# Filler matmuls of 512 columns in place of 128, and the last output tile in three column parts

## The chip, the cores and the metric

One core of one Trainium2 chip. The metric is the device time of one execution in microseconds; a profiled execution also has a span, from its first to its last recorded instruction, some 1.3 us shorter. In the lines of a profile PE is TensorE (PEld its weight loads), DVE VectorE, ACT ScalarE, POOL GpSimd and SP SyncE; a q behind the name means the engine's sequencer. A store's landing is as the profile lists it.

## The reference, cut to what matters

One transformer block on 2048 tokens of width 640: a modulated layer norm, attention with 32 heads of 128 over cached keys and values, and a second branch with a token shift and an MLP.

```python
mod = (_silu(c) @ w_mod).reshape(c.shape[0], 6, 1, -1)         # six rows of 640
h = _layernorm(x) * (1 + ca) + sa
x = x + ga * attention(h, k_cache, v_cache, wq, wo)            # 32 heads, 2048 x 2048 scores
h = _layernorm(x) * (1 + cb) + sb
x = x + gb * mixer_mlp(h, w1, w2, w3, w4)                      # ends with @ w4 (1728 x 640)
```

## The kernel before

The kernel is written as a list of operations with estimated durations. A small list scheduler in Python puts them in an order for each engine and adds the semaphores. TensorE's order is fixed by keys; the other engines' orders follow the estimates.

Fillers: matmuls of ones by ones into a bank that nobody reads, so that TensorE is busy while the first loads arrive. They are meant to keep its clock up. In the trace of before the first thirty start 107 ns apart, from 1.08 us on, and the eight at 11.58 us start 56 ns apart.

```python
def dummy(e, n, t=None):
    for _ in range(n):
        ins = e.matmul((t or warm)[:, 0:128], ones_t[:], ones_t[:], start=True, stop=True)
...
spin(30, -300)          # before the transposition of c
...
spin(26, -298)          # before the modulation product
for k in range(KT):     # the modulation product, a filler after each column for k < 2
    ...
# step 0 of attention: spin(8), the first projection, spin(9), QK, spin(9)
```

The last matmuls, one tile of 128 tokens by 640 at a time, in two halves of 320 columns:

```python
for hf in range(2):
    for f in range(NF):                                    # NF = 14
        ... matmul(m[:, hf*512 : hf*512+HD], gT[f], w4[f][:, hf*HD:(hf+1)*HD])
    if last:                                               # tile 15: finish each half at once
        ... DVE: w = m * mod5;  DVE: o_ = w + b;  SyncE: store o_
```

The end of each engine's program. The body ends with a jump to a common block, where each engine loads a flag (was any value out of range?) and branches on it:

```python
for e, eng in names.items():
    run(e, 0, n)
    hint = eng.mark_branch_hint_location()
    run(e, n, self.FIRST[e])
    eng.br("fast").branch_hint(hint)          # the jump
...
    eng.wait_ge(self.flag_op.sem, self.flag_op.semval)
    eng.load(redo[eng.engine], flag[0:1, 0:1])
    ...
    eng.br_cmp(redo[eng.engine], 0, ..., on_true="done", on_false="general")
```

The hint marks a place some 47 us before the jump, where the trace shows a BRANCH_PREFETCH_HINT (in before at 1316.19 us, with TensorE's jump at 1363.84); no run here moved it, so what it does is not shown.

## Time and profile before

| | before |
|---|---|
| time, four runs | 1367.97 us median (1367.85 to 1371.74) |
| TensorE busy | 99% of the span |
| ScalarE busy | 81% |
| last matmul's end to end of span | 2.84 us |

How to read it: TensorE carries the whole span, so time can be gained at two ends only, before its stream is dense and after its last matmul. The prediction shows the lines. A second profile of the same kernel, taken later as a control (1367.96 us), has quicker start-up loads. TensorE's waits there:

```profile
PE f_S L440 <- POOL f_ones L403: 1.0, 1, 1.0
PE f_M L465 <- DMA f_W<-in_w_mod_dram: 0.4, 2, 0.3
PE f_S L806 <- ACT f_PQ L808: 0.4, 2, 0.2
```

The waits for the K and V loads (0.7 and 0.9 us in the prediction's fence) are absent, and the wait for the modulation weights is 0.4 us in place of 1.2.

### The profile page before, as it was taken

The page shows a single profiled execution, that of the slowest core. Times are in us where ns is not written, and L with a number is a line of the kernel's source. Part 1 is how long each engine was busy: PE and PEld are TensorE (multiplying, and loading weights), DVE is VectorE, ACT ScalarE, POOL GpSimd, SP SyncE. Part 2 cuts the span into 40 slices and gives each one's busy share as a digit, 9 for nine tenths or more (in the row PEclk, how much of TensorE's full clock was granted, in tenths as well). Part 3 has the DMA queues.
Part 4 walks back from the last instruction along what each step waited for, and adds up shares of the span by engine and source line. Part 5 has one row for each costly group of instructions (what it writes and reads, how often), then busy time and mean ns, then how long its engine had stood idle before and what let it go on. Part 6 is the DMA issues. An engine that isn't in the chain of part 4 may idle for free.

```text
span 1369.3 us, 29631 instructions
## 1 busy us (share of the span) xinstructions
PE 1349.0 (99%) x12841; PEld 939.4 (69%) x13075; DVE 574.7 (42%) x1440; ACT 1103.3 (81%) x1145; POOL 111.7 (8%) x97
## 2 busy tenths in 40 slices
PE   8999999999999999999999999999999999999999
PEld 6666777677677777677677777776776776655665
DVE  5554344544323332332333233233233345799553
ACT  6988888888888888888888888888888888833322
POOL 1000000000000000000000000000233237500000
PEclk9999999999999999999999999999999999999999
DMA  9642614272335221241205121422236110441210
GB/s 211 144 97 36 115 40 81 34 130 59 81 65 90 55 48 35 48 89 33 58 10 101 36 47 36 91 54 48 55 63 136 27 15 19 114 84 44 40 43 31
DMA packets 264787, 90.38 MB, mean 66 GB/s; under 512 B 244793, under 2 KB 262266, under 8 KB 264650
## 3 DMA queue, kind: packets, MB, share of 16 engines
q1 hardware_dynamic: 260682, 84.17, 30.9%
q0 software_dynamic: 672, 2.56, 0.9%
q10 hardware_dynamic: 3296, 1.67, 0.6%
q8 instruction: 104, 1.70, 0.5%
q14 instruction: 33, 0.27, 0.1%
HBM read 41.68 MB, written 2.63 MB: 32 GB/s over the span
## 4 chain that ended last, share of the span: by engine, by line
PE 96%; DMA 1%; issue 1%; DVE 1%; ACT 0%; POOL 0%; SPq 0%; POOLq 0%
PE f_O L825 35%; PE f_S L806 29%; PE f_M L729 10%; PE f_M L760 10%; PE f_S L1002 2%; PE f_M L1002 2%; PE f_O L989 2%; PE f_S L989 2%; PE f_S L940 1%; PE f_S L963 1%; PE f_M L963 1%; DMA f_KV<-in_A_v_cache_dram 1%; PE f_O L940 1%; DMA f_W<-in_w_mod_dram 1%; PE f_O L760 0%
## 5 line engine op out<-in xcount | busy, mean ns | idle before, releaser
L808 ACT ACTIVATE f_PQ<-f_S 128x1024 bf16<-128x1024 f32 x1024 | 1042.6, 1024 | 137.5 <-PE f_S L806 105.0
L825 PEld LDWEIGHTS f_O<-f_KV,f_PQ 128*128 128x128 bf16 x8192 | 634.8, 98 | 262.3 <-DVE f_small L517 1.4
L825 PE MATMUL f_O<-f_KV,f_PQ 128*128 128x129 bf16 x8192 | 796.4, 220 | 9.3 <-DMA f_KV<-in_A_v_cache_dram 0.9
L806 PE MATMUL f_S<-f_PQ,f_KV 128*128 128x512 bf16 x1831 | 650.8, 379 | 3.2 <-DMA f_KV<-in_A_k_cache_dram 0.7
L768 DVE TENSOR_TENSOR f_y<-f_M,f_y 128x320 f32<-128x320 f32 x192 | 94.4, 492 | 465.5 <-PE f_M L760 465.5
L760 PE MATMUL f_M<-f_wo,f_OO 128*128 128x320 bf16 x992 | 272.9, 299 | 0.0
L806 PEld LDWEIGHTS f_S<-f_PQ,f_KV 128*128 128x128 bf16 x2048 | 191.6, 98 | 13.4 <-ACT f_PQ L808 2.2
L729 PE MATMUL f_M<-f_hT,f_wq 128*128 128x512 bf16 (+1 forms) x635 | 189.0, 378 | 1.8 <-DVE f_tmp L771 0.2
L760 PEld LDWEIGHTS f_M<-f_wo,f_OO 128*128 128x128 bf16 x992 | 96.3, 98 | 28.5
L834 DVE TENSOR_TENSOR f_OO<-f_O,f_rl 128x256 bf16<-128x256 f32 x256 | 108.4, 423 | 8.3
L538 POOL TENSOR_TENSOR f_y<-f_y,f_mod 128x640 f32<-128x640 f32 x32 | 49.2, 1544 | 735.2 <-DVE f_y L768 735.1
L733 DVE CAST f_PQ<-f_M 128x512 bf16<-128x512 f32 x127 | 87.8, 692 | 50.7 <-PE f_M L729 49.5
L729 PEld LDWEIGHTS f_M<-f_hT,f_wq 128*128 128x128 bf16 x640 | 62.5, 98 | 49.8 <-DVE f_tmp L771 0.6
L832 DVE RECIPROCAL f_rl<-f_O 128x2 f32<-128x2 f32 x256 | 43.5, 170 | 69.1 <-PE f_O L825 58.2
L992 ACT ACTIVATE f_OO<-f_S 128x512 bf16<-128x512 f32 x28 | 16.7, 597 | 43.6 <-PE f_S L989 43.6
L766 DVE COPY f_y<-f_M 128x320 f32<-128x320 f32 x32 | 15.7, 492 | 57.6 <-PE f_M L760 57.6
L499 DVE BATCH_NORM_STATS2 f_small<-f_y 128x6 f32<-128x320 f32 (+1 forms) x72 | 32.3, 479 | 1.0 <-POOL f_y L538 0.9
L1002 PE MATMUL f_S<-f_KV,f_OO 128*128 128x320 bf16 x224 | 31.7, 299 | 0.0
L1002 PE MATMUL f_M<-f_KV,f_OO 128*128 128x320 bf16 x224 | 31.7, 299 | 0.0
L544 ACT ACTIVATE f_xn<-f_y,f_small 128x640 bf16<-128x640 f32 x10 | 9.1, 916 | 25.7 <-DVE f_small L523 25.7
L661 DVE TENSOR_REDUCE f_small<-f_tmp 128x1 f32<-128x640 f32 x20 | 16.4, 820 | 29.9 <-ACT f_PQ L808 29.9
L992 ACT ACTIVATE f_OO<-f_O 128x512 bf16<-128x512 f32 x28 | 16.7, 596 | 14.1 <-PE f_O L989 14.1
(148 smaller groups left out, 534.9 us busy)
## 6 DMA issues: line engine op xcount, KB each, us to landing
f_KV<-in_A_v_cache_dram SPq DMA_DIRECT2D x28, 512.0 KB, 4.7
f_wo<-in_A_wo_dram SPq DMA_DIRECT2D x8, 640.0 KB, 4.3
f_wq<-in_A_wq_dram SPq DMA_DIRECT2D x7, 640.0 KB, 4.9
f_xin<-in_A_x_dram SPq DMA_DIRECT2D x13, 320.0 KB, 3.5
out_dram<-f_xin SPq DMA_DIRECT2D x15, 160.0 KB, 1.8
f_KV<-in_B_w_dram SPq DMA_DIRECT2D x5, 432.0 KB, 3.6
f_KV<-in_A_k_cache_dram SPq DMA_TRANSPOSE x128, 2.7
f_OO<-f_OO SPq DMA_TRANSPOSE x128, 2.5
```

What stands on the lines that cost most here:

```text
L538: P.op(eng, lambda e: e.tensor_tensor(out=out, in0=a, in1=b, op=op), COST[eng][0], rd, wr, prio, lat=300 if eng == "POOL" else None, dual= ...
L729: P.op("PE", lambda e, i=i, kk=kk, mm=mm, a=a, z=z: e.matmul(mm[:, 0:z - a], wq_t[g % 2][:, kk, hh * 128:(hh + 1) * 128], hT_t[ch][:, kk, ...
L733: P.op("DVE", lambda e: e.tensor_copy(q.ap, m.ap), 690, (m,), (q,), s * NP - 90)
L760: P.op("PE", lambda e, m=m, qt=qt, hf=hf, hh=hh: e.matmul(m[:, 0:HD], OT_ap[gs][:, qt, hh, :], wo_t[g % 2][:, hh, hf * HD:(hf + 1) * HD], ...
L768: P.op("DVE", lambda e, m=m, yt=yt: e.tensor_tensor(out=yt.ap, in0=m[:, 0:HD], in1=yt.ap, op=ALU.add), 490, (m, yt), (yt,), s * NP - 60)
L806: P.op("PE", lambda e, sp=sp, r=r, kt=kt: e.matmul(sp[:, r * QC:(r + 1) * QC], K_ap[b][:, kt * 128:(kt + 1) * 128], q.ap, start=True, stop ...
L808: x = P.op("ACT", lambda e, sp=sp, pt=pt: e.activation(pt.ap.rearrange("p k q -> p (k q)"), sp.ap, ACT.Exp, scale=SCALE), 1021, (sp,), (pt ...
L825: ins = e.matmul(o[bk][:, w * 129:w * 129 + 129], pt[:, r, qt * 128:(qt + 1) * 128], V_ap[b][:, u, 0:129], start=(u == 0 and w == 0), stop ...
L832: P.op("DVE", lambda e, ov=ov, i0=i0: e.reciprocal(rl_t[:, i0:i0 + 2].unsqueeze(2), ov[:, 0:258].rearrange("p (u d) -> p u d", u=2)[:, :, ...
L834: evac.append(P.op("DVE", lambda e, ov=ov, i0=i0, bk=bk: e.tensor_tensor(out=On_ap[gs][:, 2 * bk:2 * bk + 2, hh, :], in0=ov[:, 0:258].rear ...
L989: P.op("PE", lambda e, m=m, f=f, kk=kk: e.matmul(m.ap, w3_ap[:, kk, f * 128:(f + 1) * 128], nT_ap[ch][:, kk, :], start=(kk == 0), stop=(kk ...
L1002: P.op("PE", lambda e, f=f, hf=hf: e.matmul(m[:, hf * 512:hf * 512 + HD], gT_ap[:, f, i * 128:(i + 1) * 128], w4_ap[f][:, hf * HD:(hf + 1) ...
```

## The change

Its intent: a filler of 512 columns keeps the array busy as long as four of 128, with a quarter of the instructions; and the last part of the last tile is smaller, so that less VectorE work and a smaller store follow the last matmul.

```diff
-            t_eng[e] = s + (o.dur if o.dma else max(o.dur - self.LAP.get(e, 0.0), 60.0))
+            t_eng[e] = s + (o.dur if o.dma or e == "PE" else max(o.dur - self.LAP.get(e, 0.0), 60.0))
...
-            ins = e.matmul((t or warm)[:, 0:128], ones_t[:], ones_t[:], start=True, stop=True)
+            ins = e.matmul((t or warm)[:, 0:512], ones_t[:], ones_t[:].unsqueeze(1).to_broadcast([128, 4, 128]), start=True, stop=True)
...
-    spin(30, -300)
+    spin(8, -300)
...
-    spin(26, -298)
+    spin(7, -298)
...
-                if k < 2:
+                if k < 2 and j % 4 == 3:
                     dummy(e, 1)
...
-            spin(8, -271)
+            spin(2, -271)
...
-            spin(9, -100, "O0")
-            spin(9, 1.5, "O1")
+            spin(2, -100, "O0")
+            spin(2, 1.5, "O1")
...
+        if last:
+            m3 = Tile(pool="T")
+            parts = ((m, 0, 0, HD), (m, 512, HD, 512), (m3, 0, 512, D))
+        else:
+            parts = ((m, 0, 0, HD), (m, 512, HD, D))
```

The rest of the diff renames the loop over halves to one over parts.

More of the change, by code (lines that the diff above doesn't have):

```diff
@@ L444, in spin @@
         t = Tile(pool=pool) if pool else warm
-        P.op("PE", lambda e: dummy(e, n, t), n * 56, (ones,), (t,), key)
+        P.op("PE", lambda e: dummy(e, n, t), n * 216, (ones,), (t,), key)
     mc, c_ps = Tile(pool="M"), Tile(pool="M")
-    spin(30, -300)
+    spin(8, -300)
     def spread(e):
@@ L466, in mcol @@
                                start=(k == 0 and j == 0), stop=(k == KT - 1), skip_group_check=True)
-                if k < 2:
+                if k < 2 and j % 4 == 3:
                     dummy(e, 1)
             return ins
-        P.op("PE", mcol, 2 * KT * (85 if k < 2 else 62), (wm[k], s_bf, ones), (mc,) + ((warm,) if k < 2 else ()), -290 + k, accum=True)
+        P.op("PE", mcol, 2 * KT * (72 if k < 2 else 62), (wm[k], s_bf, ones), (mc,) + ((warm,) if k < 2 else ()), -290 + k, accum=True)
     saT, caT = T(small(KT)), T(small(KT))
@@ L999, in w4_tile @@
         last = t == SQ // 128 - 1
-        for hf in range(2):
+        if last:
[3 more added lines that the diff above has]
+            parts = ((m, 0, 0, HD), (m, 512, HD, D))
+        for n, (mm, o, c0, c1) in enumerate(parts):
             for f in range(NF):
-                P.op("PE", lambda e, f=f, hf=hf: e.matmul(m[:, hf * 512:hf * 512 + HD], gT_ap[:, f, i * 128:(i + 1) * 128],
-                                                                 w4_ap[f][:, hf * HD:(hf + 1) * HD], start=(f == 0), stop=(f == NF - 1)),
-                     MM(HD), (gT[f], w4_of(f), w4b, pad2), (m,), key + hf + 0.01 * f, accum=True)
+                P.op("PE", lambda e, f=f, mm=mm, o=o, c0=c0, c1=c1: e.matmul(mm[:, o:o + c1 - c0], gT_ap[:, f, i * 128:(i + 1) * 128],
+                                                                             w4_ap[f][:, c0:c1], start=(f == 0), stop=(f == NF - 1)),
+                     MM(c1 - c0), (gT[f], w4_of(f), w4b, pad2), (mm,), key + n + 0.01 * f, accum=True)
             if last:
-                c0, c1 = hf * HD, (hf + 1) * HD
-                w, o_ = tmp[t % 2], xin[3 * hf]
-                P.op("DVE", lambda e, hf=hf, c0=c0, c1=c1: e.tensor_tensor(out=w[:, c0:c1], in0=m[:, hf * 512:hf * 512 + HD], in1=mod_t[5][:, c0:c1], op=ALU.mult),
-                     490, (m, mod[5][hf]), (w,), key - 1000)
-                P.op("DVE", lambda e, o_=o_, c0=c0, c1=c1: e.tensor_tensor(out=o_[:, c0:c1], in0=w[:, c0:c1], in1=b[:, c0:c1], op=ALU.add), 490, (w, b), (o_,), key)
+                w, o_ = tmp[t % 2], xin[(0, 3, 1)[n]]
+                P.op("DVE", lambda e, mm=mm, o=o, c0=c0, c1=c1: e.tensor_tensor(out=w[:, c0:c1], in0=mm[:, o:o + c1 - c0], in1=mod_t[5][:, c0:c1], op=ALU.mult),
+                     dve(c1 - c0), (mm,) + tuple(mod[5]), (w,), key - 1000)
+                P.op("DVE", lambda e, o_=o_, c0=c0, c1=c1: e.tensor_tensor(out=o_[:, c0:c1], in0=w[:, c0:c1], in1=b[:, c0:c1], op=ALU.add),
+                     dve(c1 - c0), (w, b), (o_,), key)
                 dma("SP", lambda e, o_=o_, c0=c0, c1=c1: e.dma_start(out2d[t * 128:(t + 1) * 128, c0:c1], o_[:, c0:c1]), 80, (o_,), (), key)
```

## The prediction

> **What bounds the kernel now.** I read the page's busy shares and slices first, to see which engine carries the span and where it does not; then what TensorE waited for; then the chain of waits at the two ends, because the change touches only the start-up and the last output tile.
>
> ```profile
> PE 1349.0 (99%) x12841; PEld 939.4 (69%) x13075; DVE 574.7 (42%) x1440; ACT 1103.3 (81%) x1145; POOL 111.7 (8%) x97
> PE   8999999999999999999999999999999999999999
> PEclk9999999999999999999999999999999999999999
> ```
>
> The first line gives busy microseconds per engine: TensorE (PE) is busy 99% of 1369.3 us, ScalarE 81%. In the slices only the first is below 90%, and the granted clock is never low. The kernel is one long matmul stream, so a change pays only if it shortens that stream, shortens an idle piece of it, or shortens what follows its last matmul. TensorE's waits for the whole span:
>
> ```profile
> PE f_M L465 <- DMA f_W<-in_w_mod_dram: 1.2, 3, 0.8
> PE f_S L440 <- POOL f_ones L403: 1.0, 1, 1.0
> PE f_O L825 <- DMA f_KV<-in_A_v_cache_dram: 0.9, 1, 0.9
> PE f_S L806 <- DMA f_KV<-in_A_k_cache_dram: 0.7, 1, 0.7
> PE f_S L806 <- ACT f_PQ L808: 0.4, 2, 0.2
> ```
>
> The columns are total us, times, longest. L465 is the modulation product, L440 the fillers, L806 and L825 the two attention products. The large waits are all start-up waits, and the releaser is a transfer or the first memset, none a filler. After 60 us the same view has three waits of 0.7 us in all; from 1230 us to the end it has none. The chain through the first 30 us:
>
> ```profile
> 2.62 7.54 DMA f_W<-in_w_mod_dram
> 10.16 0.05 issue
> 10.20 0.40 PE f_M L465 x10
> ...
> 17.05 0.86 POOL f_wq L619
> 17.91 0.02 issue
> 17.93 0.01 POOLq L252
> 17.95 9.90 DMA f_KV<-in_A_v_cache_dram
> 27.85 0.14 issue
> 27.99 0.61 PE f_O L825 x8
> ```
>
> (start us, length, what). Until 10.20 us the start-up is the load of the modulation weights; from 10.2 to 17 us it is a dependent sequence; from 17.95 to 27.99 it is the load of a V head. No filler stands in it. The chain at the other end:
>
> ```profile
> 1362.62 3.82 PE f_S L1002 x28
> 1366.44 0.02 issue
> 1366.46 0.50 DVE f_tmp L1008
> 1366.97 0.02 issue
> 1366.99 0.49 DVE f_xin L1010
> ```
>
> The last tile's 28 matmuls end at 1366.44, two VectorE operations of 320 columns follow until 1367.48, and then the store, issued at 1367.51 and (by the table of transfers) 1.6 us to landing, which takes us to the end of the span at 1369.3. What is serial after the last matmul is therefore 1.02 us of VectorE and about 1.8 us of store.
>
> [...] the first 30 fillers take 3.38 us from first start to last end, so (3.38 - 0.3)/29 = 106 ns apart; later 128-column matmuls are 56 ns apart (8 fillers in 0.61 us: (0.61 - 0.22)/7), and ten of 512 columns take 2.16 us in the chain, 216 ns each. [...] 492 ns at 320 columns, 824 ns at 640. [...] The trace shows the fixed part dominating: stores of 160 KB land in 1.8 us, of 80 KB in 1.6 us. [...]
>
> **Fillers, part by part.** Columns streamed: 30 x 128 = 3840 become 8 x 512 = 4096; 26 x 128 = 3328 become 7 x 512 = 3584; 20 x 128 = 2560 inside the modulation product become 4 x 512 = 2048; 8 x 128 become 2 x 512, the same; twice 9 x 128 = 1152 become twice 1024. In all 13056 become 12800, and 102 matmuls with their weight loads become 25. Where each lies in time:
>
> - First group, cold: 8 x 427 = 3.41 us in place of 30 x 107 = 3.20. The c-transpose behind it (4.32 us in the timeline) starts about 0.2 us later, and so does the small chain to the bf16 vector, which was complete at 5.73 + 0.17 = 5.90. Its user, the first modulation product, started at 7.33 when its weights landed. 1.2 us of the 1.4 us slack stay. The VectorE work behind that chain also moves by up to 0.2 us; the last normalised tile is done at 8.57 + 1.47 = 10.04 and its transposes began at 11.30, so that is hidden too.
> - Second group: before, 2.01 us from 4.54, ending at 6.55 (part cold, part warm). After, from about 4.75: perhaps two cold and five warm, 0.85 + 1.08 = 1.9 us, ending near 6.7. The wait for the weights ends at 7.33. Hidden.
> - Inside the product: before, 20 pairs at 81 ns, 1.6 us, done by about 9.1. After, 20 products at 26 ns ((0.65 - 0.16)/19 from the 20 that follow without fillers) plus 4 x 216 = 1.38 us. The 0.2 us gained turn into waiting, since the next product waits for its weights until 9.29, and the last until 10.20.
> - The group at 11.58: 2 x 216 = 432 ns in place of 448; the projection behind it starts at 12.16, when VectorE has its first input ready at 11.56 + 0.55 = 12.11. Hidden.
> - The groups at 13.52 and 15.03: 432 in place of 504 ns each. The first is followed by QK, which waits for ScalarE's copy of q until 13.72 + 0.38 = 14.10, with fillers done at 14.02 before and 13.95 after; the second by QK at 15.88, released by the exponentials. Hidden.
>
> Sum on the path: 0.0 us. Even a gain before 17 us would have to bring the V load forward to last; it could at most be some 0.05 us.
>
> **The last tile.** Matmuls: 14 each of 320, 192 and 128 columns. 320 costs 3.80/28 = 135.8 ns in the chain; 128 about 56 (12 of 129 columns in 0.68 us in the chain); 192 by the line through these, 82.6. Sum 14 x (135.8 + 82.6 + 56) = 3.84 us against 3.80: +0.04 us. So weight loads do not bind at 128 columns: the PV stream already runs at that rate with new weights every time. [...] VectorE must be free for it: part one ends at 1365.58 as now; part two is ready at 1364.54 + 14 x 0.0826 = 1365.70 and takes 2 x 0.357 + 0.04 = 0.75 us, to 1366.47; part three's matmuls end at 1366.48. It just fits. The buffers are free: the third bank was last read by the activations that ended at 1351.85, and its output row was read by a store issued at 1361.43. The store falls from 80 to 32 KB; by the two sizes above that is an estimated -0.1 us, but its rows are 256 B[...], so I count 0. Sum of the tail: -0.36 us.
>
> **The scheduler line.** TensorE's estimated time per operation loses its floor of 60 ns. TensorE's own order is sorted by key and does not move. The only short ones are 20 transposes (58 ns, 40 ns in all) and the 14 new small ones, beside the changed estimates of the fillers. That can only flip near ties in the order of the other engines. I count 0, with a small spread either way.
>
> Sum: 1368.05 - 0.36 + 0.0 = 1367.7 us.
>
> **Rivals.**
> (1) The fillers are on the path: a quarter as many instructions free TensorE's queue, or bring the warm clock earlier, and the start-up gets shorter by up to 1 us or so (1367). For it: the first slice is the only one below 90%. Against: every wait there names a transfer or the first memset, and the fillers end before the waits do.
> (2) The clock warms later, or drops again, since the filling inside the modulation product is now in four lumps. Then transposes, projection and first QK run cold: some 2 us of matmuls between 10.2 and 16 doubled, +2 us at worst (1370). Against: the lumps are as dense, and the gaps of 0.6 us are not longer than now.
> (3) The tail gives its gain back: three stores on one queue. One of the two last stores took 1042 ns to issue, the other 333. If the middle of three takes that long from about 1366.5, the last is issued near 1367.6, later than now, and the tail gains nothing or loses 0.1 us (1368.1).
> (4) A flipped order on VectorE or ScalarE makes TensorE wait in the middle. A few waits of 0.2 to 1 us would make +1 to +3 us (1370). Against: the same rules still give nearly the same order, and ScalarE has 19% to spare. A gain by such flips is bounded by the 0.7 us of waits there.
>
> **Range and chances.** The three times before are 1367.85, 1368.05 and 1371.74: the spread of runs is ten times the effect. A range from 1366.3 to 1370.2 holds rivals 1 to 3, most of 4, and a median that meets one high run. Two per cent would be 27 us, which nothing here comes near.
>
> **What would show it.** Right: the first slice's waits still name the modulation weights, K and V loads, with the same times at 10.20 and 27.99 within 0.2 us; the fillers show as 25 matmuls; the last VectorE operations are of 128 columns, near 290 ns each, and the time from last matmul to end is about 0.4 us shorter. Wrong: a TensorE wait behind VectorE or ScalarE that was not there, a first QK later than 14.2 us, matmuls at 427 ns for 512 columns after 6 us, or a last store whose issue waits for the one before. The prediction fails if start-up changes by over 1 us or new waits in the middle exceed 2 us.

The sum came to 1368.05 - 0.36 + 0.0 = 1367.7 us, the -0.36 being +0.04 for the matmuls, -0.40 for VectorE behind the last part and 0 for the store. An estimate from the traced operations gives the same: a line through VectorE's 492 ns at 320 columns and 824 at 640 puts 128 columns at 293 ns, so 2 x 0.293 + 0.04 = 0.63 us in place of 1.02. The changed kernel's trace has 292 and 291 ns, and 358 and 359 for the 192 columns that are counted as 0.357 us. "Cold" means the pitch of the first fillers: 107 ns in before, and in after 427 ns for 512 columns up to 4.0 us, then 216 to 226 from 4.73 on. That filling brings the clock up and pauses lower it, on which rivals 1 and 2 rest, is not shown. Nor had any run then shown that rows of 256 B are slow; that became rival R below.

## The result, and the profile after

The changed kernel is correct: 1368.59 us median (1368.34 to 1370.47, four runs) against 1367.97 (1367.85 to 1371.74). The ratio is 1.0001, with a 95% interval of 0.9982 to 1.002: the same. Ratios here are the mean time of one kernel's fast runs over that of the other's fast runs of the same rounds, so not quite the ratio of the medians.

The forecast was 1367.7 with a range from 1366.3 to 1370.2, so the total is inside. But the quick runs of after (1368.34, 1368.47, 1368.71) lie some 0.6 us above those of before (1367.85, 1367.88, 1368.05), where 0.36 less was expected. TensorE's waits after:

```profile
PE f_S L440 <- POOL f_ones L403: 1.0, 1, 1.0
PE f_M L465 <- DMA f_W<-in_w_mod_dram: 0.6, 1, 0.6
PE f_S L806 <- ACT f_PQ L808: 0.5, 2, 0.3
PE f_M L963 <- ACT f_PQ L950: 0.3, 1, 0.3
PE f_S L806 <- ACT f_PQ L737: 0.3, 1, 0.3
PE f_M L729 <- DVE f_tmp L771: 0.2, 1, 0.2
```

No K or V load is waited for, as in the control of before. The chain at the end (start us, length, what):

```profile
1360.01 3.06 PE f_S L1008 x28
1363.06 0.80 PE f_O L1008 x14
1363.86 0.03 issue
1363.89 0.02 DVEq L252
1363.91 0.04 issue
1363.95 0.30 DVE f_tmp L1013
1364.26 0.02 issue
1364.28 0.29 DVE f_xin L1015
```

The last part is there: 14 matmuls in 0.80 us, two VectorE operations of 0.3 us. The last one ends at 1364.57, which is 0.73 us after the last matmul's end (1363.84), against 1.05 before. Yet the span ends at 1367.02, 3.17 us after the last matmul, against 2.84. The time is lost in the store. First before, then after, the instructions that write the output tensor, with the times that their issue took (min/median/max, ns):

```profile
L1011 SPq DMA_DIRECT2D out_dram<-f_xin x2: 333/688/1042, 1365.6 to 1367.5; - x2
DMA to landing us min/median/max: 1.6/1.6/1.6
```

```profile
L1017 SPq DMA_DIRECT2D out_dram<-f_xin x3: 332/332/1159, 1363.0 to 1364.6; - x3
```

And the view of the transfers of after, from 1362 us to the end: the instruction queue (packets, MB, share of 16 engines' time), then the stores that were issued (KB each, us from issue to landing):

```profile
q8 instruction: 1, 0.02, 0.8%
...
out_dram<-f_xin SPq DMA_DIRECT2D x1, 48.0 KB, 2.6
out_dram<-f_xin SPq DMA_DIRECT2D x1, 32.0 KB, 2.3
```

The last store took 1.6 us to land before and 2.3 us now, though it is smaller. Both kernels have one store whose issue took over 1 us. Before it was the last but one, with 0.9 us to spare; after, it is the last one. And there is one packet of 16 KB on the instruction queue (q8) in this window. The packet records of the trace put it at 1364.43 and let it last 1.01 us. Of the 128 row packets of the second store, 120 left between 1364.70 and 1365.00; the other 8 left from 1365.43, when the big packet was done, to 1365.77. Eight of 128 rows are the share of one of the 16 DMA engines that the profile counts; the records do not name the engine. The issue of the third store ended at 1365.76 and its rows left from 1366.25. By these times, then, the packet that carries instructions stood in front of the second store on one engine, and the third store stood behind the second.

Where does such a packet come from? The profile puts it on the instruction queue. The 16 KB packets of that queue lie a median of 254 traced TensorE instructions apart in before and 253 in after (near the end of before at 25529, 25785, 26038), so I take each for a block of some 256 instructions of TensorE's code. That is an estimate from the spacing. But the last packet breaks the rhythm. In before it comes after 26213 instructions, 0.71 us after TensorE's jump to the common block has finished; in after 0.74 us after it. That jump takes 0.37 us in before and 1.09 in after, where a regular packet had started 1.6 us ahead of it, 2.83 us before the last matmul's end.

**Theory L.** The length of TensorE's code decides where its packets fall. With 77 filler matmuls and 77 weight loads fewer and 28 instructions more at the end (126 in all) a regular packet falls close to the jump, the jump waits for it, and the packet behind the jump falls among the last stores. **Rivals.** F: the wide fillers themselves cost time at the start. R: rows of 384 and 256 bytes are slow stores in themselves. N: all of it is noise.

### The profile page after: what moved, and what is told of

It reads as the page before. It is cut to its first block, busy times and chain, and to the rows that moved or that the text cites. A ratio compares the mean times of both kernels' runs of the same rounds, so it can differ in the third digit from the quotient of the medians.

```text
span 1367.0 us, 29510 instructions
## 1 busy us (share of the span) xinstructions
PE 1348.4 (99%) x12778; PEld 934.7 (68%) x13012; DVE 574.7 (42%) x1442; ACT 1102.6 (81%) x1145; POOL 111.5 (8%) x97
## 3 DMA queue, kind: packets, MB, share of 16 engines
q0 software_dynamic: 672, 2.56, 0.8%
## 4 chain that ended last, share of the span: by engine, by line
PE 97%; issue 1%; DMA 1%; DVE 1%; ACT 0%; SPq 0%; DVEq 0%
PE f_O L825 35%; PE f_S L806 29%; PE f_M L729 10%; PE f_M L760 10%; PE f_M L1008 2%; PE f_O L989 2%; PE f_S L989 2%; PE f_S L1008 2%; PE f_S L940 1%; PE f_S L963 1%; PE f_M L963 1%; PE f_O L940 1%; DMA f_W<-in_w_mod_dram 0%; DMA f_hT<-f_xn 0%; PE f_S L760 0%
## 5 line engine op out<-in xcount | busy, mean ns | idle before, releaser
L1008 PE MATMUL f_S<-f_KV,f_OO 128*128 128x320 bf16 (+1 forms) x224 | 31.0, 296 | 0.0
L1008 PEld LDWEIGHTS f_M<-f_KV,f_OO 128*128 128x128 bf16 x224 | 21.9, 98 | 8.9
```

The lines of the kernel that those rows point to most:

```text
L1008: P.op("PE", lambda e, f=f, mm=mm, o=o, c0=c0, c1=c1: e.matmul(mm[:, o:o + c1 - c0], gT_ap[:, f, i * 128:(i + 1) * 128], w4_ap[f][:, c0:c1 ...
```

## The experiments

Twelve runs in three groups (ten new kernels and the two old ones again); each group ran on one chip, with runs of before between its own. All are correct. The table has the timed runs, and from each run's one profile the numbers that the argument needs. "Jump" is how long TensorE's jump took, "packet" when the 16 KB packet behind it started, from the end of the last matmul. "Store" is the last store: issue and landing, both in us from its start. "Tail" is last matmul's end to end of span.

| kernel | TensorE instr. | jump | packet | store | tail | time: median (range) | ratio to before, interval |
|---|---|---|---|---|---|---|---|
| before (first profile) | 26230 | 0.37 | -1.51 | 0.33, 1.61 | 2.84 | | |
| after (first profile) | 26104 | 1.09 | +0.58 | 1.16, 2.27 | 3.17 | | |
| before_again | 26230 | 0.36 | -1.51 | 0.33, 1.62 | 2.85 | 1370.34 (1367.96 to 1371.68) | 1.0002, 0.9988 to 1.0017 |
| after_again | 26104 | 0.94 | +0.41 | 1.37, 2.48 | 3.38 | 1369.87 (1368.84 to 1372.11) | 1.0002, 0.9988 to 1.0017 |
| tail_only | 26258 | 0.36 | -0.18 | 0.83, 1.94 | 2.85 | 1369.73 (1367.60 to 1371.87) | 0.9994, 0.9980 to 1.0009 |
| fill_only | 26076 | 3.71 | +2.47 | 0.33, 3.40 | 4.63 | 1369.15 (1368.39 to 1370.58) | 0.9995, 0.9981 to 1.0009 |
| fill_pad | 26224 | 0.38 | -1.49 | 0.33, 1.60 | 2.83 | 1368.19 (1368.04 to 1369.69) | 0.9990, 0.9977 to 1.0003 |
| before_pad | 26328 | 0.37 | -1.51 | 0.33, 1.60 | 2.83 | 1370.49 (1369.41 to 1372.22) | 1.0005, 0.9991 to 1.0018 |
| after_pad | 26252 | 0.37 | +0.23 | 0.77, 1.89 | 2.79 | 1367.71 (1367.50 to 1368.82) | 0.9986, 0.9974 to 0.9999 |
| after_late | 26105 | 0.99 | +0.47 | 1.45, 2.56 | 3.53 | 1368.81 (1368.53 to 1371.17) | 0.9992, 0.9979 to 1.0004 |
| before_pad2 | 26332 | 2.21 | +0.47 | 0.33, 1.60 | 2.83 | 1369.85 (1368.81 to 1370.22) | 1.0003, 0.9990 to 1.0016 |
| after_late2 | 26105 | 0.46 | +3.65 | 0.33, 1.45 | 3.49 | 1371.11 (1368.99 to 1373.99) | 1.0015, 1.0000 to 1.0030 |
| after_pad_late2 | 26253 | 0.37 | +3.45 | 0.33, 1.45 | 3.39 | 1368.76 (1368.47 to 1371.62) | 1.0003, 0.9989 to 1.0016 |
| split416 | 26224 | 0.37 | -0.71 | 0.33, 1.53 | 2.56 | 1368.17 (1367.38 to 1368.98) | 0.9994, 0.9981 to 1.0007 |

The instructions are those recorded in the trace. The traces of the last group hold 234 matmul records that the earlier ones lack (before has 13075 weight loads and 12841 recorded matmuls on its page); they are left out of the count here. The three groups' runs of before (11 each) had medians of 1370.03, 1370.27 and 1369.32, with single runs from 1367.54 to 1374.59.

Three things are read off at once. First, from the 65th exponential of attention to the last matmul's end every one of the 14 profiles has between 1281.34 and 1281.40 us. So nothing that any kernel here does costs or gains in the middle, and the flipped orders that the prediction feared don't exist in a size that matters. Second, all differences are in the tail (2.56 to 4.63 us) and in the start-up, up to the 65th exponential (82.0 to 86.6 us), and the start-up varies between runs of one kernel (2.6 us between the two profiles of before) by more than the tail varies between kernels (2.1 us). So the timed intervals, some 0.15% or 2 us wide to each side, do not settle the tail. The profiles do. Third, where the jump is long, it ends 2.4 to 2.8 us after the start of a regular packet (after, after_again, fill_only, after_late, before_pad2). In after_late2 such a packet had started 5.1 us before the jump, and the jump took 0.46 us. So in these profiles the jump is long where a regular packet starts less than 2 us before it or while it lasts.

One part of the start-up's spread is the clock. In before_pad the record shows half the clock from 10.44 to 13.86 us, and the transposes there start 107 ns apart, against 56 ns in the other 13 profiles; it has the latest 65th exponential of all. Of the runs with a recorded clock, 5 of 56 with narrow fillers and 5 of 50 with wide ones have a mean below 1.000, so nothing ties this to the fillers. What brings it about stays open.

### First group: the parts of the change apart

**before_again and after_again**: the two kernels unchanged.

> The kernel before, unchanged, as a control and for a second profile (its first profile fell in a run with slow start-up loads: weights landed at 10.16 us, against 9.14 in the profile of the changed kernel). All theories: ratio 1.000, fast runs near 1367.9 us, some runs 2 to 4 us longer. With quick start-up loads the span should be near 1366.6 us; the time from TensorE's last matmul to the end of the span should again be 2.84 us, and the last store again 1.6 us from issue to landing.

> The changed kernel, unchanged. In the first comparison its quick runs (1368.34, 1368.47, 1368.71) were some 0.55 us above the quick runs of before (1367.85, 1367.88, 1368.05), where I had forecast 0.36 below. If that is noise between sessions (rival), the sign is not repeated. If it is real: +0.3 to +0.7 us between quick runs. The theory of the tail: the last store again takes about 1.1 us to issue and 2.3 us to landing, the time from last matmul to the end is again about 3.17 us.

The tails repeat: 2.85, and 3.38 with a last issue of 1.37 us. The times decide nothing: the changed kernel's median lies 0.2 us below that of the eleven runs of before and 0.5 us below before_again's, while its quickest run lies 0.9 us above before_again's (1368.84 against 1367.96), all behind a start-up that spreads over 3 us. So rival N is not excluded for the difference in times; the difference in the tail repeats.

**tail_only**: the last tile in three parts, fillers of 128 columns as before.

```diff
-            ins = e.matmul((t or warm)[:, 0:512], ones_t[:], ones_t[:].unsqueeze(1).to_broadcast([128, 4, 128]), start=True, stop=True)
+            ins = e.matmul((t or warm)[:, 0:128], ones_t[:], ones_t[:], start=True, stop=True)
```

and the counts of fillers, and the scheduler line, as in before.

> The last tile in three parts, fillers and scheduler line as before. Theory T (the tail): TensorE's last two branches now come later against its last matmul, the 16 KB packet [...] (1.0 to 1.4 us on one DMA engine) falls among the last stores, the third store's issue stalls; so last matmul to end about 3.2 us in place of 2.84, and +0.3 to +0.5 us in the quick runs. Rival F (the fillers cost the time): -0.4 to 0.0 us. Rival R [...]: the same +0.3 us as theory T, but with an issue of 0.33 us and a landing of 2.3 us for the last store.

This expectation and those of the second group give the 16 KB packet behind the jump to TensorE's final branch. That was a guess from its place in the trace; after_late refutes it below. My expectation for the tail missed: it is 2.85 us, as before's. The jump is as quick as before's, the packet starts 0.18 us before the last matmul's end, and the last store takes 0.83 us to issue and 1.94 to land. The packet stands among its stores all the same: 8 rows of the first and 8 of the second left only from 1368.89 us on, when it was done. So the three parts alone gain nothing and lose nothing: what VectorE saves, the store gives back. Only with the wide fillers does the tail get longer.

**fill_only**: the wide fillers and the scheduler line, with the last tile in two halves.

```diff
-            parts = ((m, 0, 0, HD), (m, 512, HD, 512), (m3, 0, 512, D))
+            parts = ((m, 0, 0, HD), (m, 512, HD, D))
```

> The wide fillers and the scheduler line, the last tile in two parts as before. Theory T: tail as before (2.84 us from last matmul to end), time within 0.15 us of before in the quick runs. Rival F: +0.2 to +0.6 us, with a start-up that is longer in the chain (first QK later against the landing of the last modulation weights than before, where they are 3.9 to 4.0 us apart).

Missed again, and this run taught the most. Not one line at the end differs from before, and yet the tail is 4.63 us. The chain at the end, and then the transfers from 1358 us on (packets of the instruction queue; the last two stores with KB and median landing):

```profile
1360.27 3.82 PE f_S L1002 x28
1364.09 0.02 issue
1364.11 0.50 DVE f_tmp L1008
1364.61 0.02 issue
1364.64 0.49 DVE f_xin L1010
```

```profile
q8 instruction: 2, 0.03, 1.0%
...
out_dram<-f_xin SPq DMA_DIRECT2D x2, 80.0 KB, 3.4
```

The chain is that of before, instruction by instruction. What differs is the second fence: two instruction packets in the window from 1358 us on, and a last store that lands after 3.4 us. A regular packet started at 1362.45, after the jump had begun (1361.49); the jump ended at 1365.20, 2.75 us after that packet's start; the packet behind the jump lasted from 1366.54 to 1367.47, and 8 of the last store's 128 rows left only at 1367.46, over 1 us after the other 120. So with other fillers, all issued before 16 us, the end comes 1.8 us later after the last matmul in this profile; theory L puts that down to the length of the code, which the next group tests. One profile does not show that every run of fill_only has this tail. The shortest of its six spans is 1367.1 us; less 1281.34 for the middle and 4.63 for the tail, that would leave 81.1 us of start-up, and no profile here has less than 82.0. By this estimate the tail of that run was at most 3.8 us. Rival F's path, a longer start-up, is not what happened: the first exponential starts at 13.80 us, against 14.00 in before_again.

### Second group: the length of the code alone

**fill_pad, before_pad, after_pad**: idle instructions on TensorE, one by one before operations in the attention stream, where they turn out to cost nothing (the middle keeps its 1281.34 to 1281.40 us). They wait for a semaphore that has long been reached.

```diff
+                if e == "PE" and a == 0 and k >= 1000 and (k - 1000) % 20 == 0 and (k - 1000) // 20 < 154:
+                    for by in ("POOL", "DVE")[:1 if waits[o] else 2]:
+                        eng.wait_ge(sems[by], 1)
```

(By the traces' counts 148 instructions are added in fill_pad and after_pad, 98 in before_pad with 102 in place of 154.)

> Wide fillers, last tile in two parts, and 148 idle wait instructions spread one by one over TensorE's attention stream, so that its code is again about as long as before's. Theory L (code length decides where TensorE's 16 KB instruction packets fall): the last packet but one falls again some 190 instructions before the end, the jump at the end takes 0.36 us (fill_only: 3.71), the packet of the final branch comes 1.5 us before the last matmul, the last store lands in 1.6 us, last matmul to end 2.85 us (fill_only: 4.63). At the start, as in fill_only: first packet near 14 us, last modulation weights near 9.05 us, first exponential near 13.8. Time: below before by 0.2 to 2 us, as before's start-up is slow or quick. Rival (the wide fillers themselves spoil the tail, say by the clock or the order of other engines): tail stays near 4.6 us.

> The kernel before, nothing of the change, only 98 idle wait instructions more in TensorE's attention stream, which brings the next packet boundary to some 20 to 50 instructions before the end, as in fill_only. Theory L: the jump at the end takes 1 to 3.7 us, the final branch's packet comes 0.4 to 2.5 us after the last matmul, among the last stores; last matmul to end 3.2 to 4.7 us in place of 2.85; time +0.3 to +1.9 us. Start-up as before: first packet at 8.6 to 9.5 us. Rival (packets have nothing to do with it): tail 2.85, time as before.

> The changed kernel with 148 idle waits more on TensorE, so with the wide fillers' start-up and with tail_only's place of the packets. Theory L: jump 0.36 us, final branch's packet 0.2 us before the last matmul's end, last store issue 0.83 and landing 1.94 us, tail 2.85 (after: 3.17 and 3.38). So 0.3 to 0.5 us below the changed kernel, and below before by 0.2 to 2 us. Rival: tail as in after.

fill_pad came out as expected: tail 2.83 against 4.63 in fill_only, jump 0.38 against 3.71, and no other line of the kernel differs from fill_only (the two ran in different groups, on different chips). Its transfers from 1358 us on:

```profile
q8 instruction: 1, 0.02, 0.4%
...
out_dram<-f_xin SPq DMA_DIRECT2D x2, 80.0 KB, 1.6
```

So neither the fillers' own work nor the scheduler line, which fill_pad has too, makes the long tail. after_pad is shorter too, as expected: 2.79 against 3.17 and 3.38. It is also the only kernel whose interval lies below 1 (0.9974 to 0.9999), 0.14% faster than before in that group; among twelve such intervals, one that just misses 1 may be chance. before_pad missed: its tail is 2.83, with no regular packet near the jump. It was four instructions short, since fill_only's 26076 plus a block of 256 (25529 to 25785 in before) is 26332 and it had 26328.

**after_late**: TensorE's final branch waits for the last three stores.

```diff
             eng.load(redo[eng.engine], flag[0:1, 0:1])
+            if e == "PE":
+                for o in [o for o in self.seq["SP"] if o.dma][-3:]:
+                    eng.wait_ge(o.sem, o.semval)
```

> The changed kernel, but TensorE's final branch waits until the last three stores have landed, so that the packet it fetches cannot fall among them. Theory C (the packet holds up the stores): last store issue 0.33 us, landing 1.4 to 1.6 us, last matmul to end 2.3 to 2.6 us in the profile, in place of 3.17 and 3.38; measured time below the changed kernel by 0.5 to 0.8 us if the late packet hides behind the end of the program, else no gain. Rival R (rows of 384 and 256 bytes are slow in themselves): last store still 2.0 to 2.5 us to landing.

A wrong idea of mine fell here: the packet still came 0.47 us after the last matmul and the tail was 3.53 (the last store landed at 3.31; TensorE's own final branch ends the span). The packet does not belong to the final branch. In the kernels of these groups it follows the end of the jump to the common block, by 0.7 to 0.9 us, 1.1 in after_pad and split416 and 1.34 in fill_only. This run says nothing of rival R.

### Third group: the mirror, the packet out of the way, and another split

**before_pad2**: before_pad with 102 idle instructions in place of 98.

> As before_pad, but with 102 idle waits on TensorE in place of 98. before_pad showed no packet near the end; fill_only (26076 traced TensorE instructions) did, and 26076 + 256 = 26332, four more than before_pad's 26328. With 102 the count is 26332. Theory L (the length modulo 256 decides): the tail of fill_only, without any part of the change: jump at the end 2.5 to 3.7 us (before 0.36), the packet behind it 1 to 2.5 us after the last matmul, last matmul to end 3.2 to 4.7 us (before 2.85). Rival: 2.85 again. Start-up as before's.

Half right. Four instructions more, and a regular packet is there (2.77 us before the last matmul's end), the jump takes 2.21 us in place of 0.37, and the packet behind it comes 0.47 us after the last matmul in place of 1.51 before it. No part of the change is in this kernel. But the tail stays 2.83: the packet ended at 1366.86, before the last store's rows left at 1367.33. So theory L holds for the jump and the packet; whether the stores suffer depends on a gap of half a microsecond, which I had not worked out.

**after_late2 and after_pad_late2**: the waits stand before the jump.

```diff
+            if e == "PE":
+                for o in [o for o in self.seq["SP"] if o.dma][-3:]:
+                    eng.wait_ge(o.sem, o.semval)
             eng.br("fast").branch_hint(hint)
```

> As after_late, with the waits put before TensorE's first jump, since after_late showed that the packet follows that jump by 0.7 us, not the final branch. Theory C (the packet holds up the last stores): none among them now; last store issue 0.33 us, landing 1.4 to 1.6 us, last matmul to the end of SyncE's stream 2.3 to 2.5 us; the profile's span may then end with TensorE's own jump and flag load, some 1 us after the landing. Measured time: below the changed kernel by up to 0.8 us if the end of the program doesn't wait for TensorE, above it by up to 1 us if it does. Rival R (short rows are slow): landing still above 2 us.

> after_late2 with the 148 idle waits of after_pad. Stores as in after_late2; TensorE's jump takes 0.36 us, its end comes some 1 us after the last landing. If the program's end waits for it, 0.0 to 0.5 us above after_pad, else 0.3 us below it.

The instructions of after_late2 that write the output tensor, with the times of their issue, and then its transfers from 1358 us on, with KB and landing:

```profile
L1020 SPq DMA_DIRECT2D out_dram<-f_xin x3: 332/332/333, 1364.8 to 1366.4; - x3
```

```profile
out_dram<-f_xin SPq DMA_DIRECT2D x1, 48.0 KB, 1.5
out_dram<-f_xin SPq DMA_DIRECT2D x1, 32.0 KB, 1.5
```

All three issues take 0.33 us, and rows of 384 and of 256 bytes land in 1.5 us. That settles rival R for these stores: the short rows do not land later. SyncE's stream ends 2.35 us after the last matmul, 0.5 us less than in before, which is what the change was made for (and 0.8 to 1.0 less than the changed kernel's 3.17 and 3.38). But TensorE's late jump now ends last (3.49), and the times are no better: 1371.11 with a slow start-up, and 1368.76 with the padding, against 1368.17 for split416 in the same group. The end waits for TensorE: where SyncE's stream ends last, the measured time is 1.32 to 1.41 us longer than that stream in the profile; here it is 2.70 us longer than SyncE's stream, and 1.57 us longer than TensorE's.

**split416**: two parts of 416 and 224 columns, wide fillers, 148 idle instructions.

```diff
-            parts = ((m, 0, 0, HD), (m, 512, HD, 512), (m3, 0, 512, D))
+            parts = ((m, 0, 0, 416), (m, 512, 416, D))
```

> The wide fillers, last tile in two parts of 416 and 224 columns, and 148 idle waits. [...] last store 1.6 us from issue to landing, packet 1.1 to 1.2 us before the last matmul's end and so ahead of the last store: last matmul to end 2.6 to 2.7 us. Against after_pad (2.79): 0.1 to 0.2 us less, against before 0.2 in the tail and 0.2 to 2 us in the start-up. It may be the fastest of all kernels here.

The chain at the end of its profile:

```profile
1359.70 3.82 PE f_S L1010 x28
1363.51 0.02 issue
1363.54 0.40 DVE f_tmp L1015
1363.94 0.02 issue
1363.96 0.39 DVE f_xin L1017
```

VectorE's part after the last matmul is 0.85 us (0.82 was expected), the store of 56 KB lands in 1.53 us, the packet (from 0.71 us before the last matmul's end, 0.93 us long) is over before the last store's rows leave. The tail is 2.56 us, the shortest of all, and the span of 1366.06 is the shortest too. In the times it is 1368.17 against 1369.32 for before in its group, with an interval that holds 1. By the spans of the profiles it and after_pad are the best kernels here, by the ratios after_pad and fill_pad; the gain over before, about 0.1%, is shown for after_pad only, and just so.

## Why the prediction was right or wrong, point by point

**The total: right, by the width of its range.** The median rose by 0.62 us where a fall of 0.36 was forecast. The range of 3.9 us was set by the spread of the runs, so the total says nothing for the mechanism. Of the signs that the prediction named, the VectorE operations of 128 columns (0.29 us each) came, and so did one sign of being wrong, a last store whose issue waits. The start-up moved by over 1 us, which it had called failure (65th exponential at 85.06 us before, 82.47 after); but before_again has the same quick start without the change.

**The fixed part of a store: shown in part.** Landing took 1.8 us for 160 KB and 1.6 for 80, so half the bytes took off 0.2 us. What the rest is made of is not shown; of the 1.61 us of before's last store, 0.36 come after the end of its last packet.

**What bounds the kernel, and the scheduler line: right.** The middle is the same to 0.06 us in all profiles.

**The fillers' own time: right where it could be read.** The transposition of c moved from 4.32 to 4.53 us (0.2 forecast). The filled part of the product took 1.38 us, from 7.01 to 8.39, exactly the sum. The projection, the first QK and the fillers between them waited for the same things as before.

**"Sum on the path: 0.0 us": the step that failed.** It counted the fillers as array time and let 77 matmuls and their weight loads vanish for nothing. They are 154 instructions of code, and the 16 KB instruction packets come every 253 or 254 traced instructions (median). Taking them out moved the last packets against the end of the program. In the profile of fill_only, where only the fillers and the scheduler line differ, this cost 1.8 us in the tail, and in fill_pad 148 idle instructions gave it back. In the changed kernel the same effect is part of the 0.3 to 0.5 us.

**The last tile's -0.36 us: wrong in sign.** Its terms: matmuls +0.04 forecast, +0.04 measured (3.86 against 3.82 us). VectorE -0.40 forecast; it measured -0.32, from 1.05 to 0.73, since the pair of operations is as short as computed but starts 0.11 us after the last matmul in place of 0.03 (VectorE is busy with the second part until 1363.85; the prediction had said that "it just fits"). The store 0 forecast, +0.66 and +0.87 measured against 1.61. That is the term of the sum that was mis-sized: at after_late2 the same store takes 1.45 us, so 0.8 to 1.0 us of its 2.27 and 2.48 are the instruction packet and what queues behind it.

**Rival 3 came true, without its cause.** The prediction had seen an issue of 1042 ns in the profile of before and had asked what happens if the last store meets it. It put the loss at 0.1 us and took the long issue for a trait of the queue. The instruction packet at 1364.91 us stood in the same trace.

**Rivals 1, 2 and 4.** Rival 4 (waits in the middle) did not happen. Rival 2 (a cold clock) is in none of the nine profiles with wide fillers, where the transposes run 56 ns apart; the one profile that shows it, before_pad's, has narrow ones. Rival 1 (a shorter start-up) stays half open. Over the 14 profiles the last modulation weights landed at 9.2 to 10.2 us with narrow fillers (five) and at 9.0 to 9.7 with wide ones (nine); the 65th exponential started at 84.9 us on average against 82.9 (before_pad's cold stretch is in the first mean). The first 16 KB packet came at 8.7 to 10.5 us with narrow fillers and at 13.2 to 14.2 with wide ones, so the wide fillers go with a first packet that comes after the weights' load. But the quickest narrow start (82.45) is about as quick as the wide ones, the weights' own rows were mostly through before the packet began, and no experiment here moved the packets at the start with the fillers kept. Fewer fillers may save some 1 to 2 us of start-up in many runs; why is not settled. It could explain why fill_only was no slower than before in spite of a tail that was 1.8 us longer in its profile; so could a shorter tail in its other runs.

So in the tail the expected gain of 0.36 us came back as a loss of 0.3 to 0.5 us. Whether the start-up gains anything is not settled, and the times (ratios of 1.0001 and 1.0002, intervals 0.15 to 0.2% wide to each side) are too coarse to show either.

## What to carry to other kernels

The 148 idle TensorE instructions of fill_pad cost nothing in the middle (1281.34 to 1281.40 us in every profile), yet with them the tail was 2.83 us in place of 4.63. In these kernels of 26000 TensorE instructions the packets of code stood among the stores: before trusting a gain of less than a microsecond at the end of a program, look for instruction packets among the last stores. To test for it, add idle instructions in the dense part, where they cost nothing here, and see whether the tail moves. And when one store in a profile takes three times as long to issue as its neighbours (1042 against 333 ns in before), find out what stood in its way before building on it.

## What these runs measured of instruction packets and small stores

- A 16 KB packet of the instruction queue lasted 0.9 to 1.4 us near the end of these runs (2.1 us once in the start-up of after). In the middle their place made no difference (1281.34 to 1281.40 us, idle instructions or not). Among the last stores, 8 of a store's 128 rows left only when the packet was done, and a following store's issue took 1.16 to 1.45 us (after, after_again, after_late) in place of 0.33. The last store landed 0.4 us (after_pad: 1.89 against 1.45 in after_late2) to 1.8 us (fill_only: 3.40 against 1.60 in fill_pad) later.
- TensorE's jump took 0.36 to 0.46 us with no regular packet started in the 5 us before it, and 0.94 to 3.71 us in five profiles, where it ended 2.4 to 2.8 us after the start of a regular packet.
- For the landing of these small stores short rows cost nothing: 32 KB in rows of 256 B landed in 1.45 us, 48 KB in rows of 384 B in 1.51, 80 KB in rows of 640 B in 1.60 to 1.62. The rate while the rows leave does fall, from some 210 GB/s (80 KB in 0.39 us) to 121 GB/s (32 KB in 0.27 us) in after_late2.
- Two kernels with the same last instructions differed by 1.8 us in the tail (fill_only against before_again), and 148 idle instructions took that away (fill_pad).
